# Preparing a batch's keys and values at separate places in the attention plan

## The chip, the cores and the metric

The kernel runs on one core of a Trainium2 chip. The metric is the device time of one execution in microseconds. A core has TensorE (PE, matrix products, with PEld as its weight loads), VectorE (DVE), ScalarE (ACT), GpSimd (POOL) and SyncE (SP, which here issues nearly all DMAs). Each engine takes its instructions in the order in which they were put into its queue, and waits at the head of the queue for what the instruction needs.

## The reference

Attention with keys and values that are averaged over groups of 8 positions, and an FFN behind it:

```python
k_p = k.reshape(B, H, Sp, 8, D).mean(axis=3)      # B=8, H=8, S=576, D=64, Sp=72
v_p = v.reshape(B, H, Sp, 8, D).mean(axis=3)
scores = scale * q @ k_p.T;  attn = softmax(scores);  x = attn @ v_p
x = x.transpose(0, 2, 1, 3).reshape(4608, 512)
h = x @ w_in                                      # 512 -> 2048
out = (h * clip(h + 3, 0, 6) / 6) @ w_out         # 2048 -> 512
```

## The kernel before

The 4608 tokens are cut into ten blocks of 512, 256, 384, six times 512 and 384 tokens. `run` does one block's FFN in 16 steps, one for each 128 columns of d_ff: `h` (12 matmuls into a PSUM tile `psh`, L774), `relu` on ACT and `gate` on DVE (L782, L786), `hi` on ACT and `lo` on DVE, which split the result into two fp32r parts `ghi` and `glo` (L790, L794), and two steps later `out` (L803), which adds into one PSUM tile `pso` per 128 tokens. After the last step the sums go through ACT into tiles `o` and out by DMA (L806, L808). So block 1 is a run of narrow matmuls of 256 columns, block 2 of 384, the others of 512.

While block j's FFN runs, the attention of block j+1 is fed in between its matmuls. `block_steps(j)` makes a list of attention steps for a block: for each tile of 128 tokens and each group of four heads one "scores" step (`scores`: products L412, maximum L416, exponentials L420, reciprocal of the sum L436 and L437, division on POOL L448 and L454), a transposing step three scores steps behind (`transposes`: L518, L520, then `ahi`, `alo`, `arem` by ACT and DVE, L529 to L541), and at the end of a batch's part four "av" steps (`av`, L583, which give `x`). `split_x` (L561, L562) splits x before the next block. `Paced` spreads a block's list evenly over the slots that the FFN's matmuls offer.

What the attention needs of a batch is made by side steps, which `side_steps(b)` lists. For the keys: four loads (`load_k`, L200, 288 KB each into `kst`) and four `prep_k` (a DVE reduction to `ksum`, L214, and two ACT copies into the tile `kbd`, L222). For the values: six loads (`load_v` and `load_vr`, L228 and L233; the last two are three DMAs each) and six `prep_v` (DVE reductions into `vsum`, L332; then the placing into `vhi`, `vlo` and `vrem` by ACT and DVE, L345 to L360, with two POOL memsets ahead, L318). The q tiles are loaded one tile ahead (`load_q`, L193).

`plan` joins the lists of blocks 2 to 9 into one list `every`, and hangs the side steps of batches 2 to 7 on its entries, to be done ahead of the entry. Batches 0 and 1 are prepared by hand at the start. `kbd` and the value tiles have two buffers, by the batch's parity.

Several tiles share one ring of four buffers of 128 x 576 fp32 (`ring`): raw keys, raw values, the value sums `vsum` (held from a batch's first to its last value reduction), the second half of a q tile that spans two batches (with a POOL memset, L192), and the output tiles `o`.

A scheduler puts each engine's instructions into its queue by the program's order and by when it believes them ready. Up to the fourth FFN step of block 1 the order is instead written out by hand, in `ORDER`, as numbers of an engine's instructions in program order (SP's list holds its DMAs), and `put_in_order` ties them.

Of the kernel before, what the change touches and what calls it, by code (L numbers as in the profile page):

```python
# [23 lines left out]

TLAG = 3

SIDE = 20

WSCALE = 2.0**8

# [28 lines left out]
        93 62 90 85 87 94 117-120 91 126-129 99 102 92 115 103 100 112 136 65 130 137 101 138-139 116 113 124  # L59
        121 114 125 122 140 123 143 66 63 131 64 132 134 144 135 153 133 145 141 147 142 150 148 146 154 151 149  # L60
        155 157 160 156 152 166 158 161 159 167 170-172 162-163 168 164 173 165 174 176 178 169 175 183 177
        180-181 179 187 186 184 188 185 194-197 189 202-205 198-199 182 200 208-211 190-191 201 206-207 192
        212-213 193
    """,
    "Pool": """
# [1 line left out]
    """,  # L67
    "SP": """
        2-3 1 0 4-5 8 6-7 14 9 11 10 22-24 21 20 13 12 15 18 16 19 25-26 28 31 17 27 32 34 33 29 41 30 44 51 35
        48 46 43 36 47 39 52 59 42 37-38 45 40 50 49 53-55 57-58 60-62 64 63 56  # L70
    """,
}

# [2 lines left out]
def attention_moe_kernel(  # L76
# [34 lines left out]
    for j, t in enumerate(starts):  # L111
        end, mine = t + BLOCKS[j], []
        while t < end:
            n = min(end, (t // S + 1) * S, t + (256 if j == 0 else end)) - t
# [83 lines left out]
    def load_k(b, p):  # L198
        kraw[b, p] = ring("kst")
        nc.sync.dma_start(kraw[b, p], k[b, p])  # L200
# [3 lines left out]
    def prep_k(b, p):  # L204

        two = b == 0
        if not two:
            ks = pool.tile([P, 1, SP], F32, name="ksum", bufs=1)
        elif p % 2 == 0:
            ks = ksum[p // 2] = piece(0, 2 * SP).rearrange("p (i s) -> p i s", i=2)  # L210
        else:
            ks = ksum[p // 2]
        i = p % 2 if two else 0
        nc.vector.tensor_reduce(  # L214
            out=ks[:, i], in_=kraw.pop((b, p)).rearrange("p (s o) -> p s o", o=POOL), axis=AX.X, op=ALU.add
        )
        if i == two:

            scale = 1.0 / (POOL * D**0.5)
            for h in range(2):  # L220
                rows = slice(h * D, (h + 1) * D)
                nc.scalar.mul(kbds[b % 2][rows, p - i : p + 1, h * SP : (h + 1) * SP], ks[rows], scale)  # L222
# [3 lines left out]
    def load_v(b, p):  # L226
        vraw[b, p] = ring("vst")
        nc.sync.dma_start(vraw[b, p][:, : POOL * D], v[b, p])  # L228

    def load_vr(b, g):  # L230
        vraw[b, NPAIR + g] = ring("vst")
        for c in range(3):
            nc.sync.dma_start(vraw[b, NPAIR + g][c * REM : (c + 1) * REM, : POOL * D], vr[b, g])  # L233
# [88 lines left out]
    def prep_v(b, p):  # L322


        if p == 0:
            if b not in W:
                place_v(b)
            sums = ring("vsum")[:, : (NPAIR + NG) * D]
            vsum[b] = sums.rearrange("p (c d) -> p c d", d=D)
        n = P if p < NPAIR else 3 * REM  # L330
        vs, st = vsum[b], vraw.pop((b, p))
        nc.vector.tensor_reduce(  # L332
            out=vs[:n, p], in_=st[:n, : POOL * D].rearrange("p (o d) -> p d o", o=POOL), axis=AX.X, op=ALU.add
        )
        if p == NPAIR - 1:
            place_heads(b, vs[:, :NPAIR])
        elif p == NPAIR + NG - 1:
            place_rest(b, vs[:, NPAIR:])
# [253 lines left out]
    def side_steps(b):  # L592

        ks = [lambda p=p: load_k(b, p) for p in range(NPAIR)]
        ks += [lambda p=p: prep_k(b, p) for p in range(NPAIR)]
        vs = []
        n = NPAIR + NG
        for p in range(n + 2):
            if p < n:
                vs.append(lambda p=p: load_v(b, p) if p < NPAIR else load_vr(b, p - NPAIR))  # L600
            if p >= 2:
                vs.append(lambda p=p: prep_v(b, p - 2))
        return ks, vs
# [5 lines left out]
    def block_steps(j):  # L609


        todo, steps, left = [], [], list(parts_of[j])

        def turn():
            tile, g = todo.pop(0)
            steps.append(([], lambda: transposes(j, tile, g), None, ()))
            if g == NG - 1:
                while left and (left[0][0], left[0][1] + left[0][2]) in [(b, s0 + n) for b, s0, n, _ in tile]:
                    pb, _, T, x0 = left.pop(0)
                    steps.extend(([], lambda p=p, a=(j, pb, x0, T): av(*a, p), "av", (pb,)) for p in range(NPAIR))  # L620

        for t in tiles_of[j]:
            pre = loads_behind(t)
            for g in range(NG):
                steps.append((pre, lambda t=t, g=g: scores(j, t, g), "scores", [x[0] for x in t]))
                pre = []
                todo.append((t, g))
                if len(todo) > TLAG:
                    turn()
        while todo:  # L630
            turn()
        return steps
# [259 lines left out]
    b = [Scores(t, g) for g in range(NG) for t in B]  # L892
# [77 lines left out]
    def plan():  # L970


        every = []
        for j in range(2, len(BLOCKS)):
            later_steps[j] = block_steps(j)
            every += later_steps[j]
        for b in range(2, NB):
            ends = [n for n, x in enumerate(every) if x[2] and b - 2 in x[3]]
            begin = max(ends) + 1 if ends else 0
            end = min(n for n, x in enumerate(every) if x[2] == "scores" and b in x[3])  # L980
            begin = max(begin, end - SIDE)
            ks, vs = side_steps(b)
            for n, x in enumerate(ks + vs):
                every[begin + n * (end - begin) // len(ks + vs)][0].append(x)

    plan()

    def run(steps, lag, attention, first_slot=0, preps={}):
# [88 lines left out]
```

## Time and profile before

| | |
|---|---|
| runs | 928.81 us median of 3 (928.56 to 930.24) |
| profiled execution | 929.94 us, span 928.2 us |
| PE busy | 910.8 us (98%) |
| DVE, ACT, POOL busy | 456.0 (49%), 460.3 (50%), 78.0 us (8%) |
| mean granted clock of TensorE | 0.996 |
| DMA | 57.17 MB, 62 GB/s mean |

The span is the time from the first to the last instruction; the rest of an execution lies around it. A busy share is a mean over the whole span; a stage is read from the rows of its own stretch. In a row of a timeline, the bracket holds the idle time of the engine before the instruction and what ended it.

### The profile page before, as it was taken

What the parts mean: (1) busy time and instruction counts of PE and PEld (TensorE: products, weight loads), DVE (VectorE), ACT (ScalarE), POOL (GpSimd) and SP (SyncE); (2) the same over time, 40 slices, a digit from 0 to 9 for tenths busy, and PEclk for the clock granted to TensorE, in tenths of its full rate; (3) what the DMA queues carried; (4) which work ended last, traced back from release to release, by engine and by line L of the source; (5) the groups of instructions that cost most, each with busy time, mean ns of one, the idle gap of its engine ahead of it and who ended that gap; (6) DMA issues with size and microseconds to landing.
All of it is one profiled execution on the core that took longest, in us unless ns stands there. A gap on an engine that the chain in (4) does not pass through costs nothing.

```text
span 928.2 us, 12551 instructions
## 1 busy us (share of the span) xinstructions
PE 910.8 (98%) x4500; PEld 775.8 (84%) x4500; DVE 456.0 (49%) x915; ACT 460.3 (50%) x1340; POOL 78.0 (8%) x167
## 2 busy tenths in 40 slices
PE   7899998999999999999999999999999999999997
PEld 7788887999887888888888888888888888888996
DVE  6999846564358532744354325733454224332321
ACT  5998665574446534544364435533544244333322
POOL 4100001021001100101011100110011001000000
PEclk9999999999999999999999999999999999999999
DMA  9960205040015000400050003200200000000100
GB/s 306 392 242 3 89 12 171 25 124 18 1 41 159 12 12 32 151 12 6 1 168 15 12 1 115 78 12 1 74 24 12 1 34 25 0 1 7 40 1 34
DMA packets 41790, 57.17 MB, mean 62 GB/s; under 512 B 7552, under 2 KB 23424, under 8 KB 41728
## 3 DMA queue, kind: packets, MB, share of 16 engines
q1 hardware_dynamic: 41584, 56.37, 18.9%
q8 instruction: 35, 0.57, 0.3%
q14 instruction: 27, 0.22, 0.1%
q10 hardware_dynamic: 144, 0.00, 0.0%
HBM read 46.93 MB, written 9.44 MB: 61 GB/s over the span
## 4 chain that ended last, share of the span: by engine, by line
PE 91%; DVE 3%; DMA 3%; ACT 1%; issue 1%; SPq 1%; ACTq 0%; DVEq 0%
PE psh L774 41%; PE pso L803 41%; PE psa L583 4%; PE psa L412 4%; PE psa L518 1%; DMA kst<-k_l 1%; DVE vsum L332 1%; DMA stage<-v_l 1%; PE psa L290 1%; DMA vst<-v_l 1%; DVE ksum L214 0%; PE psa L520 0%; DVE mx L416 0%; ACT o L806 0%; DMA out<-o 0%
## 5 line engine op out<-in xcount | busy, mean ns | idle before, releaser
L774 PE MATMUL psh<-xhi,w 128*128 128x512 f32 (+2 forms) x1288 | 403.3, 373 | 0.2
L803 PE MATMUL pso<-w,ghi 128*128 128x512 f32 x1152 | 363.5, 397 | 0.0
L774 PEld LDWEIGHTS psh<-xhi,w 128*128 128x128 f32 x1288 | 238.3, 189 | 37.3 <-DVE g L786 0.7
L803 PEld LDWEIGHTS pso<-w,ghi 128*128 128x128 f32 x1152 | 209.7, 188 | 36.2
L774 PE MATMUL psh<-xlo,w 128*128 128x512 f32 (+2 forms) x644 | 237.7, 369 | 0.0
L786 DVE SCALAR_TENSOR_TENSOR g<-g,psh 128x512 f32<-128x512 f32 (+2 forms) x161 | 101.4, 630 | 272.2 <-ACT g L782 271.6
L803 PE MATMUL pso<-w,glo 128*128 128x512 f32 x576 | 223.0, 393 | 0.5 <-DVE glo L794 0.5
L782 ACT ACTIVATE g<-psh,small 128x512 f32<-128x512 f32 (+2 forms) x161 | 103.7, 644 | 218.1 <-PE psh L774 204.3
L774 PEld LDWEIGHTS psh<-xlo,w 128*128 128x128 f32 x644 | 121.6, 189 | 18.6
L794 DVE TENSOR_TENSOR glo<-g,ghi 128x512 fp32r<-128x512 f32 (+2 forms) x161 | 103.4, 642 | 60.2 <-ACT ghi L790 59.0
L790 ACT CAST ghi<-g 128x512 fp32r<-128x512 f32 (+2 forms) x161 | 92.9, 577 | 76.3 <-DVE g L786 72.7
L803 PEld LDWEIGHTS pso<-w,glo 128*128 128x128 f32 x576 | 108.1, 188 | 23.3 <-DVE glo L794 0.9
L420 ACT ACTIVATE e<-psa,mx 128x72 f32<-128x72 f32 x256 | 78.5, 321 | 45.9 <-DVE mx L416 45.0
L448 POOL TENSOR_TENSOR a<-e,sm 128x256 f32<-128x256 f32 x60 | 38.1, 635 | 508.8 <-DVE sm L437 232.4
L420 ACT ACTIVATION_READ_ACCUMULATOR e<-psa,mx 128x1 f32 x256 | 52.6, 205 | 0.0
L412 PEld LDWEIGHTS psa<-kbd,qt 128*128 128x128 f32 x288 | 43.6, 191 | 4.4 <-issue 0.2
L416 DVE TENSOR_REDUCE mx<-psa 128x4 f32<-128x288 f32 x72 | 32.5, 454 | 29.2 <-PE psa L412 28.8
L412 PE MATMUL psa<-kbd,qt 128*128 128x144 f32 x288 | 46.0, 287 | 0.0
L332 DVE TENSOR_REDUCE vsum<-vst 128x64 f32<-128x512 f32 (+1 forms) x36 | 37.7, 1065 | 6.0 <-DMA vst<-vr_l 2.6
L585 ACT COPY x<-psa 128x192 f32<-128x192 f32 (+7 forms) x60 | 22.9, 387 | 31.7 <-PE psa L583 31.4
L529 ACT CAST ahi<-psa 128x256 fp32r<-128x256 f32 (+1 forms) x70 | 24.4, 350 | 25.1 <-PE psa L518 12.7
L530 DVE TENSOR_TENSOR alo<-psa,ahi 128x256 fp32r<-128x256 f32 (+1 forms) x70 | 27.4, 393 | 17.4 <-ACT ahi L529 16.7
(92 smaller groups left out, 611.4 us busy)
## 6 DMA issues: line engine op xcount, KB each, us to landing
out<-o SPq DMA_DIRECT2D x36, 256.0 KB, 2.3
raw<-w_in_l SPq DMA_DIRECT2D x16, 512.0 KB, 8.5
raw<-w_out_l SPq DMA_DIRECT2D x16, 512.0 KB, 9.2
kst<-k_l SPq DMA_DIRECT2D x28, 288.0 KB, 3.9
qt<-q_l SPq DMA_DIRECT2D x28, 256.0 KB, 3.3
vst<-v_l SPq DMA_DIRECT2D x24, 256.0 KB, 3.1
vst<-vr_l SPq DMA_DIRECT2D x36, 64.0 KB, 2.0
stage<-k_l SPq DMA_DIRECT2D x4, 288.0 KB, 3.7
```

Of the source, the lines that this page charges most:

```text
L332: nc.vector.tensor_reduce(out=vs[:n, p], in_=st[:n, : POOL * D].rearrange("p (o d) -> p d o", o=POOL), axis=AX.X, op=ALU.add)
L412: nc.tensor.matmul(to, qt[:, p, :], kbds[b % 2][:, p, :], start=r == 0, stop=r == last)
L416: nc.vector.tensor_reduce(out=self.mx, in_=self.ps, axis=AX.X, op=ALU.max, negate=True)
L420: nc.scalar.activation(self.e[:, h], self.ps[:, h], AF.Exp, bias=self.mx[:, h : h + 1], accum_out=self.sm[:, h : h + 1])
L448: engine.tensor_tensor(out=self.a[:, : 4 * D].rearrange("p (h s) -> p h s", h=4), in0=e[:, :, :D], in1=sm[:, :, None].broadcast_to([P, 4, D]),
L583: nc.tensor.matmul(ps, l, r, start=n == 0, stop=n == len(mms) - 1)
L774: nc.tensor.matmul(self.ps, l[f][:, c, :], r[:, c, :], start=c == 0 and i == 0, stop=c == NCC - 1 and i == 2)
L782: nc.scalar.activation(self.g, self.ps, AF.Relu, bias=half, scale=1.0 / (6.0 * WSCALE))
L786: nc.vector.scalar_tensor_tensor(out=g, in0=g, scalar=1.0, in1=self.ps, op0=ALU.min, op1=ALU.mult)
L790: nc.scalar.copy(self.ghi, self.g)
L794: nc.vector.tensor_tensor(out=self.glo, in0=self.g, in1=self.ghi.bitcast(F32), op=ALU.subtract)
L803: nc.tensor.matmul(pos, l, r[f], start=f == 0 and i == 0, stop=f == NF - 1 and i == 2)
```

## The change

The side steps of a batch are no longer one list of 20 that ends at the batch's first scores. The eight key steps are spread over the 12 entries before the batch's first scores entry, and the twelve value steps from that entry to the batch's first av entry. Each part begins no earlier than behind the last scores (for keys) or the last av (for values) of the batch two before. In the stretch that is ordered by hand, the four key loads of batch 2 drop out of SP's list (numbers 61 to 64 are gone, and 60 is then the q load), and on ACT instruction 192 goes ahead of 207.

```diff
-SIDE = 20
+SIDE = 12
...
-        180-181 179 187 186 184 188 185 194-197 189 202-205 198-199 182 200 208-211 190-191 201 206-207 192
+        180-181 179 187 186 184 188 185 194-197 189 202-205 198-199 182 200 208-211 190-191 201 206 192 207
         212-213 193
...
-        48 46 43 36 47 39 52 59 42 37-38 45 40 50 49 53-55 57-58 60-62 64 63 56
+        48 46 43 36 47 39 52 59 42 37-38 45 40 50 49 53-55 57-58 60 56
...
+        def uses(kind, b):
+            return [n for n, x in enumerate(every) if x[2] == kind and b in x[3]]
+
         for b in range(2, NB):
-            ends = [n for n, x in enumerate(every) if x[2] and b - 2 in x[3]]
-            begin = max(ends) + 1 if ends else 0
-            end = min(n for n, x in enumerate(every) if x[2] == "scores" and b in x[3])
-            begin = max(begin, end - SIDE)
-            ks, vs = side_steps(b)
-            for n, x in enumerate(ks + vs):
-                every[begin + n * (end - begin) // len(ks + vs)][0].append(x)
+            begin = uses("scores", b)[0]
+            for side, kind, begin, end in zip(
+                side_steps(b), ("scores", "av"), (begin - SIDE, begin), (begin, uses("av", b)[0])
+            ):
+                begin = max([begin] + [n + 1 for n in uses(kind, b - 2)])
+                for n, x in enumerate(side):
+                    every[begin + n * (end - begin) // len(side)][0].append(x)
```

## The prediction

> **What bounds the kernel now.** I read the page's busy times first, then the stretches of each FFN block, then two of these stretches instruction by instruction.
>
> ```profile
> span 928.2 us, 12551 instructions
> PE 910.8 (98%) x4500; PEld 775.8 (84%) x4500; DVE 456.0 (49%) x915; ACT 460.3 (50%) x1340; POOL 78.0 (8%) x167
> ```
>
> ```profile
> 138.00:186.00 48.00, 45.59 (x276) 40.91 (x275) 28.58 (x67) 25.64 (x84) 5.09 (x11) 0.96 0.31 95
> 186.00:262.00 76.00, 76.00 (x404) 69.13 (x403) 34.72 (x81) 40.23 (x134) 8.88 (x20) 1.00 0.15 44
> 262.00:360.00 98.00, 96.68 (x459) 79.71 (x458) 51.33 (x105) 45.40 (x147) 8.48 (x18) 1.00 0.18 53
> 360.00:459.00 99.00, 99.00 (x472) 82.78 (x471) 46.37 (x94) 46.60 (x144) 9.05 (x19) 1.00 0.15 47
> ```
>
> The window rows give length, then PE, PEld, DVE, ACT and POOL busy time, the granted clock, DMA share and GB/s; the four are the runs of FFN blocks 1 (256 tokens), 2 (384), 3 and 4 (512 each). PE is the bound, and none of its matmuls changes, so only its idle time and its clock can move. After the start-up it is idle in two of these rows alone: 48.00 - 45.59 = 2.41 us in block 1 and 98.00 - 96.68 = 1.32 us in block 3; block 1 also has the one reduced clock. Everything that can be won lies there, and a loss would be a new gap elsewhere. The first gap, closer:
>
> ```profile
> 156.00:158.00 2.00, 0.87 (x4) 0.38 (x2) 1.94 (x5) 0.78 (x3) 0.00 (x0) 1.00 0.37 91
> 158.00:160.00 2.00, 0.75 (x5) 0.59 (x6) 1.94 (x4) 1.69 (x9) 0.00 (x0) 1.00 0.50 142
> 160.00:162.00 2.00, 2.00 (x12) 2.00 (x11) 2.00 (x6) 1.33 (x4) 0.81 (x2) 0.51 0.32 94
> 162.00:164.00 2.00, 2.00 (x10) 1.81 (x9) 1.94 (x4) 0.64 (x2) 0.05 (x1) 0.63 0.08 16
> ```
>
> ```profile
> 155.06 1.07 DVE L332 TENSOR_REDUCE vsum<-vst 128x64 f32<-128x512 f32 x1 [2.33 <-DMA vst<-v_l]
> 156.47 1.03 DVE L332 TENSOR_REDUCE vsum<-vst 128x64 f32<-128x512 f32 x1
> 157.79 1.00 DVE L332 TENSOR_REDUCE vsum<-vst 128x64 f32<-128x512 f32 x1
> 158.82 0.29 DVE L541 TENSOR_TENSOR arem<-psa,arem 32x128 fp32r<-32x128 f32 x1
> 159.25 0.41 PE L518 MATMUL psa<-ident,a 128*128 128x128 f32 x2 [2.38 <-DVE arem L541]
> ```
>
> A timeline row is start, length, engine, line, operation, and in brackets the idle time before and who ended it. DVE stood 2.33 us at the head of its queue for batch 2's first values, and then did three value reductions (1.07 + 1.03 + 1.00) before the arem that frees PE. That is 5.43 us of value work ahead of arem, for a PE gap of 2.38 us, so PE had a lead of about 3.05 us over DVE here (an estimate from these rows). Behind the gap the clock is 0.51 and 0.63 for 2 us each: 2 x 0.49 + 2 x 0.37 = 1.72 us lost.
>
> The second gap, in block 3:
>
> ```profile
> 190.71 1.95 SPq L200 DMA_DIRECT2D kst<-k_l  x3
> 192.72 0.42 SPq L228 DMA_DIRECT2D vst<-v_l  x1
> ...
> 199.14 0.33 SPq L228 DMA_DIRECT2D vst<-v_l  x1
> ```
>
> ```profile
> 194.62 0.31 POOL L192 MEMSET qt<- 128x256 f32 x1 [0.91 <-DVE ksum L214]
> 272.20 3.02 DVE L332 TENSOR_REDUCE vsum<-vst 128x64 f32<-128x512 f32 x3 [0.62 <-PE psa L412]
> 279.50 1.09 ACT L806 ACTIVATE o<-pso 128x512 f32<-128x512 f32 x2
> 282.26 0.34 SPq L200 DMA_DIRECT2D kst<-k_l  x1
> 288.47 0.75 DVE L214 TENSOR_REDUCE ksum<-kst 128x72 f32<-128x576 f32 x1 [3.31 <-DMA kst<-k_l]
> 289.88 0.96 PE L803 MATMUL pso<-w,glo 128*128 128x512 f32 x3 [0.51 <-DVE glo L794]
> ```
>
> Here I read the ring of four buffers that raw keys, raw values, the value sums, the second half of a two-batch q tile and the output rows share. At 194.62 the q half-tile of the tile that spans batches 2 and 3 takes a slot, which its scores give back only at about 272. Three raw values of batch 3 (from 192.72 to 199.14) hold the others, so their sum finds no slot until 272.20. Block 2's outputs, later in program order, are copied only from 279.50. Batch 4's keys queue behind the outputs (282.26), DVE stands 3.31 us for them, glo is late and PE waits.
>
> **The change, part by part.** First the price of what is moved.
>
> ```profile
> L332 DVE TENSOR_REDUCE vsum<-vst 128x64 f32<-128x512 f32 x24 | 24.9, 1064 | 3.2 <-DMA vst<-v_l 2.5 <-PE psa L412 0.6
> L332 DVE TENSOR_REDUCE vsum<-vst 96x64 f32<-96x512 f32 x12 | 12.8, 1065 | 2.8 <-DMA vst<-vr_l 2.6
> L359 ACT ACTIVATE vrem<-vsum,small 96x128 fp32r<-96x128 f32 x24 | 7.7, 392 | 4.5 <-DVE vsum L332 4.5
> L360 DVE SCALAR_TENSOR_TENSOR vrem<-vsum,small,vrem 32x128 fp32r<-32x128 f32 x24 | 6.8, 336 | 0.2
> L346 DVE SCALAR_TENSOR_TENSOR vlo<-vsum,vhi 64x256 fp32r<-64x256 f32 x12 | 5.1, 423 | 1.9 <-POOL vlo L318 1.7
> L345 ACT ACTIVATE vhi<-vsum 64x256 fp32r<-64x256 f32 x12 | 5.0, 415 | 0.8 <-DVE sm L436 0.6
> ```
>
> *Nothing is added or removed; places move.* Per batch the values cost DVE 4 x 1.064 + 2 x 1.065 + 2 x 0.423 + 4 x 0.336 = 8.58 us, ACT 2 x 0.415 + 4 x 0.392 = 2.40 us, ten DMAs on SP (four L228, six L233) and two memsets on POOL (L318). Counting the steps of the planned list from 0 (0 to 15 run beside block 1's FFN, 16 to 35 beside block 2's), batch 2's values leave steps 6 to 15 for steps 16 to 30. Its keys go from steps 0 to 5 to steps 4 to 14. Later batches shift by some 8 to 14 steps in the same way, so that values of one batch lie beside the keys of the next.
>
> *Block 1.* DVE falls from 28.58 to 28.58 - 8.58 = 20.0 of 48 us. The wait of 2.33 us and all reductions ahead of arem go with the values. Gain: 2.38 us of PE idle and 1.72 us of clock, 4.10 in all. What is late next is the first keys:
>
> ```profile
> 142.04 5.52 SPq L200 DMA_DIRECT2D kst<-k_l  x4
> 147.65 0.56 SPq L193 DMA_DIRECT2D qt<-q_l  x1
> 148.26 0.61 SPq L808 DMA_DIRECT2D out<-o  x1
> 164.23 0.35 SPq L200 DMA_DIRECT2D kst<-k_l  x1
> ```
>
> ```profile
> 146.45 0.75 DVE L214 TENSOR_REDUCE ksum<-kst 128x72 f32<-128x576 f32 x1 [1.31 <-DMA kst<-k_l]
> ```
>
> In SP's written order the four key loads drop out, so the q load and the held-back output pass them: the keys start 0.56 + 0.61 = 1.17 us later, at about 143.2. DVE's wait for the first ksum, 1.31 us now without a PE gap, becomes some 2.5 us; queued behind it are that block's max, gate and lo operations, and PE waits for those. 2.5 is under the lead of 3.05, so nothing at best. If the load took as long as the one issued at 282.26, whose ksum starts 6.21 us later, DVE would stand until 149.4, which is 4.3 us from the 145.14 at which it fell idle (146.45 - 1.31). Minus 3.05 that is 1.2 us of PE idle. I take the middle, 0.6 us lost, because the order of DVE behind the written stretch is made anew with the loads later in it.
>
> *Block 2.* It gets 8.58 us of DVE work, 34.72 + 8.58 = 43.3 of 76 us (57%, against 60% in block 1 now), under a PE with no idle. It also gets the ten loads on SP among the q loads, and the two POOL memsets among the divisions, where POOL has 8.88 of 76 us. The lead should grow with the matmul's width: 3.05 x 384/256 = 4.6 us (estimate). One wait of 2.33 us with one reduction (1.07) stays below it; the whole old burst of 5.43 us would exceed it by 0.8 us, and with a clock drop cost 2.5 us. Bounds 0 and 2.5; I take 0, because this stretch already takes six loads of batch 3 in its first 13 us (190.71 to 199.14, above) with PE 76.00 of 76.00 busy.
>
> *Block 3.* In program order batch 3's values now come behind block 2's outputs, so they no longer hold three slots beside the q half-tile (that slots are granted in program order is my reading of the rows, no row says it). The outputs get theirs at once, and the reductions from 272.20 on are those of batch 3's values and batch 4's keys (6 + 4 = 10) instead of 6 + 4 + 6 = 16. Block 4's run has ten at its start now, four ksum and six vsum, and no idle:
>
> ```profile
> 374.08 0.75 DVE L214 TENSOR_REDUCE ksum<-kst 128x72 f32<-128x576 f32 x1
> ...
> 388.16 1.07 DVE L332 TENSOR_REDUCE vsum<-vst 96x64 f32<-96x512 f32 x1
> ```
>
> Gain 1.32 us, bounds 0 and 1.32.
>
> *Later blocks, and the rest of the written order.* They have no idle time to give and get the same ten reductions per block in another order: 0. One output copy on ACT goes ahead of one ghi cast in block 1: at most one copy's length, 0.55 us (1.09 / 2), inside the lead: 0.
>
> The sum: -2.38 - 1.72 - 1.32 + 0.6 = -4.8 us. The profiled execution took 929.94 us, its span and 1.74 us around it, and would come to 925.1. It lies 1.13 us above the median of the runs, 928.81, which comes to 924.0.
>
> The clock term deserves a doubt. The row shows half clock right behind a gap of 2.38 us. The Trainium skill, page "TensorE: Matmul & The Clock Gate", Part 1, says that the clock halves after an idle window of about 3.4 us and comes back after as much busy time; the stretch at half clock fits the second half, the gap is shorter than the first. By the page alone the dip would need another cause, and the time would be 925.7; the row has no second candidate, so I keep the 1.72.
>
> **The rivals.**
> 1. *One stall of the old size comes back*, on the first keys in block 1 or on the values in block 2. For it: DVE's waits stand at 1.31 and 3.31 us on keys already, and DVE takes its work in order. Against it: the leads above. It needs a DVE delay over 3.05 us (block 1) or 4.6 us (block 2). 924.0 - 0.6 + 4.10 = 927.5: no measurable change.
> 2. *Slower: the ring starves the values in block 2.* Value sum and q half-tile hold two of four slots, so eight loads (the last values and batch 3's keys) pass two at a time, and DVE stands before one reduction after the other. It decides where two reductions in a row each wait over 2.33 us, so that wait and work pass the 4.6 us of lead twice. Two stalls at 4.10: 923.4 + 8.2 = 931.6. Against it: the values are needed only at the last four of block 2's twenty steps.
> 3. *It doesn't do what it says.* DMA queues are not paced by steps: a batch-3 key load, due in block 2's run, goes out at 164.23 already. If values still went out and were reduced in block 1: 928.8.
> 4. *Block 3's gap stays*, because batch 4's keys still land late: 924.0 + 1.32 = 925.3.
> 5. *The clock dip isn't the gap's child* and stays: 924.0 + 1.72 = 925.7.
>
> **How the numbers follow.** My forecast 0.55, rival 1 0.14, rival 2 0.12, rival 3 0.05, rival 4 0.09, rival 5 0.05. A difference of 0.2% (1.86 us) is about what can be told from none: faster means below 926.95. So faster 0.55 + 0.09 + 0.05 = 0.69, same 0.14 + 0.05 = 0.19, slower 0.12. The range runs from the full gain without the 0.6 (923.4, and some 0.6 for scatter: 922.8) to rival 1 with 0.5 of scatter (928.0); it leaves out rivals 2 and 3.
>
> **What would show it.** Right: no vsum in 138 to 186; PE 48 of 48 busy there and clock 1.00; block 2's output copies before 272; no ksum wait over 3 us near 285. Wrong: a PE gap "<-DVE" or a second half-clock stretch in 140 to 215, with a ksum or vsum waiting for its DMA just before it.

## The result and the profile after

The changed kernel took 923.10 us (median of 6 runs, 922.26 to 926.27); the kernel before took 929.33 us in the same comparison (6 runs, 927.67 to 930.71). The ratio is 0.9937, with an interval of 0.9919 to 0.9956: 6.2 us less, where 4.8 were forecast. The profiled execution took 926.27 us, its span and 2.05 us around it, and is the slowest of the six, for a reason that lies in the start-up and is shown below.

The busy times of after, and then its stretches of blocks 1, 2 and 3, with the columns length, PE, PEld, DVE, ACT and POOL busy, granted clock, DMA share, GB/s:

```profile
span 924.2 us, 12571 instructions
PE 909.7 (98%) x4500; PEld 775.6 (84%) x4500; DVE 456.8 (49%) x915; ACT 461.8 (50%) x1340; POOL 80.9 (9%) x167
```

```profile
138.00:186.00 48.00, 48.00 (x307) 43.59 (x306) 22.95 (x60) 26.16 (x84) 6.15 (x13) 1.00 0.21 64
186.00:262.00 76.00, 76.00 (x404) 68.99 (x404) 41.30 (x93) 40.80 (x136) 8.27 (x18) 1.00 0.20 56
262.00:360.00 98.00, 98.00 (x468) 81.93 (x467) 46.57 (x96) 46.25 (x145) 8.51 (x18) 1.00 0.15 46
```

PE is busy for the whole of every row. The idle 2.41 us of block 1 and 1.32 us of block 3 are gone, the clock is 1.00 in block 1 (before 0.96), and no gap has come in their place in these rows.

The amounts are read better from one instruction that both kernels do equally often. Every FFN step has a gate (L786) that comes behind PE's sums for the step. There are 161 in each kernel, 17 in block 0 (one of its steps is done in two halves) and 16 in each other block, so the 17th, 33rd, 49th and 65th are the last of blocks 0 to 3. Timeline rows of the 17th, 49th, 65th and last gate, first of before, then of after:

```profile
124.02 0.68 DVE L786 SCALAR_TENSOR_TENSOR g<-g,psh 128x512 f32<-128x512 f32 x1
259.24 0.55 DVE L786 SCALAR_TENSOR_TENSOR g<-g,psh 128x384 f32<-128x384 f32 x1 [3.19 <-ACT g L782]
359.63 0.69 DVE L786 SCALAR_TENSOR_TENSOR g<-g,psh 128x512 f32<-128x512 f32 x1 [4.98 <-ACT g L782]
917.80 0.55 DVE L786 SCALAR_TENSOR_TENSOR g<-g,psh 128x384 f32<-128x384 f32 x1 [2.49 <-ACT g L782]
```

```profile
127.25 0.68 DVE L786 SCALAR_TENSOR_TENSOR g<-g,psh 128x512 f32<-128x512 f32 x1
257.94 0.56 DVE L786 SCALAR_TENSOR_TENSOR g<-g,psh 128x384 f32<-128x384 f32 x1 [3.19 <-ACT g L782]
355.93 0.69 DVE L786 SCALAR_TENSOR_TENSOR g<-g,psh 128x512 f32<-128x512 f32 x1 [4.99 <-ACT g L782]
914.28 0.55 DVE L786 SCALAR_TENSOR_TENSOR g<-g,psh 128x384 f32<-128x384 f32 x1 [2.49 <-ACT g L782]
```

After minus before is +3.23 at the 17th, still in block 0's FFN, then -1.30, -3.70 and -3.52. So the profiled execution of after lost 3.23 us ahead of everything that the change touches (two kernels below that leave this part as it was, with the later q load alone and with the second try beside it, lost 3.17 and 2.96 us there in theirs); blocks 1 and 2 gained 4.53, block 3 gained 2.40, and the remaining six blocks gave back 0.18 (-3.70 to -3.52). The sum over the touched part is -6.75 us, close to the -6.2 of the medians; the two profiled executions differ only by 3.67 because of the start-up. That part is in these rows of after:

```profile
34.00:36.00 2.00, 1.01 (x3) 0.84 (x3) 2.00 (x5) 1.92 (x4) 0.00 (x0) 0.66 1.07 351
36.00:38.00 2.00, 2.00 (x6) 1.59 (x5) 2.00 (x3) 1.50 (x4) 0.00 (x0) 0.50 1.03 397
38.00:40.00 2.00, 2.00 (x7) 1.72 (x7) 0.95 (x3) 1.15 (x4) 0.00 (x0) 0.50 1.03 412
40.00:42.00 2.00, 2.00 (x7) 1.53 (x7) 2.00 (x4) 1.56 (x4) 0.00 (x0) 0.63 1.02 408
```

Half clock from about 34.6 to 41.5 costs 0.68 + 1.00 + 1.00 + 0.74 = 3.42 us. In before's profile the clock is 1.00 in these four stretches, and its half clock of the start-up falls at 12 to 18 us (0.82, 0.50 and 0.83 in its three rows), where it delayed little: the profiled execution with two added reductions below, whose clock is 1.00 over all of the first 46 us, has its 17th gate only 0.41 us earlier. Single executions are therefore set against each other below by differences of gates, and kernels by their medians.

### The profile page after: what moved, and what is told of

The parts are those of the page before. It is cut to its first block, busy times and chain, and to the rows that moved or that the text cites. A ratio compares the mean times of both kernels' runs of the same rounds, so it can differ in the third digit from the quotient of the medians.

```text
span 924.2 us, 12571 instructions
## 1 busy us (share of the span) xinstructions
PE 909.7 (98%) x4500; PEld 775.6 (84%) x4500; DVE 456.8 (49%) x915; ACT 461.8 (50%) x1340; POOL 80.9 (9%) x167
## 4 chain that ended last, share of the span: by engine, by line
PE 96%; DMA 3%; DVE 1%; issue 0%; ACT 0%; SPq 0%; ACTq 0%; DVEq 0%
PE psh L774 43%; PE pso L803 43%; PE psa L583 4%; PE psa L412 4%; PE psa L518 2%; DMA raw<-w_in_l 1%; DMA raw<-w_out_l 1%; DMA stage<-k_l 1%; PE psa L520 0%; SPq L257 0%; ACT stage L420 0%; DVE u L700 0%; DVE u L689 0%; DVE stage L448 0%; ACTq L1078 0%
## 5 line engine op out<-in xcount | busy, mean ns | idle before, releaser
L803 PE MATMUL pso<-w,ghi 128*128 128x512 f32 x1152 | 364.9, 397 | 0.0
L803 PEld LDWEIGHTS pso<-w,ghi 128*128 128x128 f32 x1152 | 209.5, 188 | 36.1
L786 DVE SCALAR_TENSOR_TENSOR g<-g,psh 128x512 f32<-128x512 f32 (+2 forms) x161 | 101.4, 630 | 271.9 <-ACT g L782 270.8
L803 PE MATMUL pso<-w,glo 128*128 128x512 f32 x576 | 223.0, 392 | 0.0
L803 PEld LDWEIGHTS pso<-w,glo 128*128 128x128 f32 x576 | 108.2, 188 | 22.3
L448 POOL TENSOR_TENSOR a<-e,sm 128x256 f32<-128x256 f32 x60 | 40.3, 673 | 517.0 <-PE pso L803 180.3
L436 DVE TENSOR_SCALAR sm<-sm 128x4 f32<-128x4 f32 x72 | 12.7, 180 | 48.9 <-ACT e L420 45.1
```

The lines of the kernel that those rows point to most:

```text
L448: engine.tensor_tensor(out=self.a[:, : 4 * D].rearrange("p (h s) -> p h s", h=4), in0=e[:, :, :D], in1=sm[:, :, None].broadcast_to([P, 4, D]),
L786: nc.vector.scalar_tensor_tensor(out=g, in0=g, scalar=1.0, in1=self.ps, op0=ALU.min, op1=ALU.mult)
L803: nc.tensor.matmul(pos, l, r[f], start=f == 0 and i == 0, stop=f == NF - 1 and i == 2)
```

## The experiments

The theory after the result: two stalls, each of DVE standing in its queue before work that PE does not need yet, made up the whole gain. The rivals: the amount of DVE work in a narrow block, and the spreading of preparation as such, a little for each batch. An instruction that is tied behind another comes after it in its engine's queue. All ratios are to the kernel before, run in the same comparison.

**Only the later batches apart** (batch 2 with the loop body of before, batches 3 to 7 as in the change).

```diff
+        for b in [2]:
+            ...
-        for b in range(2, NB):
+        for b in range(3, NB):
             begin = uses("scores", b)[0]
```

> Batch 2 is prepared as before (keys and values together, in block 1's run); batches 3 to 7 as after the change. Theory (two separate gaps): block 1's gap of 2.4 us stays, with or without 1.7 us of half clock behind it; block 3's goes, because batch 3's values now come behind block 2's outputs: 1.3 to 1.8 us less than before, 927.5 to 928.0. Rival A (too much DVE work in the narrow block 1): the same here. Rival B (the gain is that bursts of key and value loads are spread out, in every block): five of six batches are spread, so five sixths of the 6.2 us, about 924.2.

Measured: 928.33 us against 929.91, ratio 0.9979 (0.9967 to 0.9991), 1.6 us less. Its stretches of blocks 1 and 3, and its 49th and 65th gate:

```profile
138.00:186.00 48.00, 45.08 (x274) 40.64 (x274) 28.59 (x67) 25.18 (x83) 5.09 (x11) 0.96 0.31 95
...
262.00:360.00 98.00, 98.00 (x469) 82.06 (x469) 46.22 (x97) 46.17 (x146) 8.54 (x18) 1.00 0.15 46
```

```profile
259.87 0.56 DVE L786 SCALAR_TENSOR_TENSOR g<-g,psh 128x384 f32<-128x384 f32 x1 [3.19 <-ACT g L782]
357.86 0.69 DVE L786 SCALAR_TENSOR_TENSOR g<-g,psh 128x512 f32<-128x512 f32 x1 [4.99 <-ACT g L782]
```

Block 1 keeps its stall (2.92 us idle and a clock of 0.96), block 3 is full. Against before the gates go from +0.63 to -1.77: block 3 alone is worth 2.40 us again, and five of six batches apart bring only that. A share for each batch would have been five sixths of 6.2 us; that rival falls.

**Block 3's stall by one load.** Before, with the q load of tile 13 (the tile with a half in the ring) hung ten steps later.

```diff
                 every[begin + n * (end - begin) // len(ks + vs)][0].append(x)
+        every[35][0].append(every[25][0].pop(0))
```

> The kernel before, with one edit: the load of the q tile that spans batches 2 and 3 is hung ten steps later (35 instead of 25), behind batch 3's value loads, so its second half no longer holds a ring slot while batch 3's values are prepared. Theory: batch 3's value sums then run in block 2 near 200 to 215 instead of at 272, block 2's outputs are copied near 266, block 3's idle of 1.32 us goes, block 1's gap stays: 927.5 to 928.0. Rival B (bursts): keys and values are loaded together as before, so nothing is won: 929.3. If the late q half itself holds up the first scores of block 3, PE gets a new gap near 262 and the time is 929 to 931.

Measured: 929.32 us, ratio 0.9989 (0.9978 to 1.0001): no gain that can be told. The mechanism is there all the same:

```profile
186.00:262.00 76.00, 75.44 (x399) 68.32 (x399) 39.91 (x91) 40.00 (x136) 8.69 (x20) 1.00 0.18 53
262.00:360.00 98.00, 98.00 (x469) 82.05 (x468) 46.24 (x96) 45.81 (x146) 9.12 (x18) 1.00 0.15 46
```

```profile
209.71 1.04 DVE L332 TENSOR_REDUCE vsum<-vst 96x64 f32<-96x512 f32 x1
211.27 0.44 PE L774 MATMUL psh<-xhi,w 128*128 128x384 f32 x1 [0.56 <-DVE g L786]
270.27 1.58 ACT L806 ACTIVATE o<-pso 128x512 f32<-128x512 f32 x3 [1.26 <-PE pso L803]
```

One q load moved behind the values, and no value or key step: block 3 is full, batch 3's values are reduced within block 2 (the last at 209.71), and block 2's outputs are copied from 270.27 instead of 279.50. So the slot of the q half-tile did hold up the values, and they the outputs and batch 4's keys. But three of the reductions now stand ahead of the gate at 210.68 in block 2, and PE is idle for 0.56 us there, so a part of the gain is given back: by the gates block 3 gains 2.41 us and block 2 loses 1.10.

**Block 1's stall by its queue, first try.** Before, with the first reduction of batch 2's values tied behind tile 6's second arem.

```diff
-        )
+        ); (b, p) == (2, 0) and behind(traced[-1], arem[all_tiles[6]])
...
-                )
+                ); arem[tile] = traced[-1].name
```

> The kernel before, with one edit: batch 2's first value reduction on DVE is tied behind the arem of the tile that is being transposed, so DVE does not stand before the late values with arem behind it. All value work stays in block 1. Theory: the 2.38 us gap near 157 goes, and the half clock behind it where it falls; block 3's gap stays: 2.4 to 4.1 us less than before, 925.2 to 926.9. Rival A (too much DVE work in block 1, 28.6 of 48 us): the wait only moves and PE is as late a little later, 928.5 to 929.5. Rival B (bursts of loads): no change, 929.3.

Measured: 929.65 us, ratio 0.9993 (0.9981 to 1.0005). It missed, and DVE's rows tell why:

```profile
156.22 1.06 DVE L332 TENSOR_REDUCE vsum<-vst 128x64 f32<-128x512 f32 x1 [2.42 <-DMA vst<-v_l]
157.31 0.29 DVE L541 TENSOR_TENSOR arem<-psa,arem 32x128 fp32r<-32x128 f32 x1
157.63 1.05 DVE L332 TENSOR_REDUCE vsum<-vst 128x64 f32<-128x512 f32 x1
...
159.09 1.00 DVE L332 TENSOR_REDUCE vsum<-vst 128x64 f32<-128x512 f32 x1
160.01 0.41 DVE L786 SCALAR_TENSOR_TENSOR g<-g,psh 128x256 f32<-128x256 f32 x1
160.47 0.58 PE L774 MATMUL psh<-xhi,w 128*128 128x256 f32 x1 [1.86 <-DVE g L786]
```

Only one reduction was tied, and the next took its place at the head of the queue. DVE still stood 2.42 us, and three reductions still came ahead of the gate at 160.01: 0.49 us of PE idle before the arem and 1.86 before the gate took the place of 2.38 at the arem.

**Both single edits together** gave as little:

> The edits of the last two together, on the kernel before; keys and values of each batch stay together. Theory: both gaps go without the change, so the time is that of the changed kernel within 1 us: 923.1 to 924.5. Rivals A and B: most of the gap to the changed kernel remains, 927 to 929.

Measured: 929.40 us, ratio 0.9996 (0.9983 to 1.0009). It missed too. Block 3 is full again (98.00 of 98 us), but block 1 has 45.70 of 48 at a clock of 0.96, as with the first try, and block 2 has 75.43 of 76, as with the later q load.

**Block 1's stall by its queue, second try.** Every reduction of batch 2's values is tied behind the glo that was written last before it in program order; all of them stay in block 1.

```diff
-        )
+        ); b == 2 and behind(traced[-1], late[0])
...
-            nc.vector.tensor_tensor(out=self.glo, ..., op=ALU.subtract)
+            nc.vector.tensor_tensor(out=self.glo, ..., op=ALU.subtract); late[:] = [traced[-1].name]
```

> The kernel before, with all six reductions of batch 2's values left in block 1 but each held in VectorE's queue behind the glo that was traced last before it, so that the first of them comes after tile 6's arem, mx and a gate and none stands before unlanded values ahead of what TensorE needs. All work stays in block 1. Theory (the wait in the queue, not the amount of work): TensorE's gap of 2.4 us in block 1 goes, and with it the half clock behind it; block 3's gap stays. That is 2.4 to 4.1 us less than before: 925.5 to 927.6, ratio 0.9955 to 0.9975. Rival A (too much VectorE work for the narrow block of 256 tokens): a gap of 1.5 us or more stays in block 1, 928.5 to 930, ratio 0.9985 to 1.001.

Measured: 925.21 us against 929.48, ratio 0.9950 (0.9935 to 0.9966), 4.3 us less. Its three stretches, and the start of its value work:

```profile
138.00:186.00 48.00, 47.98 (x299) 43.33 (x298) 29.89 (x69) 27.95 (x88) 6.03 (x13) 1.00 0.32 95
186.00:262.00 76.00, 75.48 (x401) 68.31 (x401) 35.18 (x81) 38.97 (x134) 7.80 (x18) 1.00 0.15 44
262.00:360.00 98.00, 97.41 (x460) 80.47 (x459) 53.49 (x107) 47.00 (x149) 8.49 (x18) 1.00 0.18 53
```

```profile
153.55 0.28 DVE L541 TENSOR_TENSOR arem<-psa,arem 32x128 fp32r<-32x128 f32 x1
154.16 0.29 DVE L541 TENSOR_TENSOR arem<-psa,arem 32x128 fp32r<-32x128 f32 x1 [0.33 <-ACT arem L540]
157.07 1.07 DVE L332 TENSOR_REDUCE vsum<-vst 128x64 f32<-128x512 f32 x1
```

This is the clearest run. DVE does more in block 1 than before (29.89 us in that stretch against 28.58), and PE is full, at full clock: the two arem go first, and the reduction at 157.07 finds its data there and waits for nothing. The amount of work in the narrow block was not the matter; that rival falls. The time came out 0.3 us below the expected range. By the gates block 1 alone gained 4.48 us, more than the 4.1 that its idle time and its clock promised; block 3, which lost less than before (0.59 us idle against 1.32), gained 1.01, and block 2, where a gate now comes late (0.52 us idle), lost 0.85.

**That and the later q load together.**

> The kernel before with both single edits: batch 2's six reductions held behind a glo each, and tile 13's query loads hung at step 35 in place of step 25. No preparation moves to another block by program order. Theory (two stalls make up the whole gain): both gaps go, a gap of about 0.5 us appears in block 2 as it did with the query loads alone, and the time comes within 1.5 us of the changed kernel: 923 to 926, ratio 0.993 to 0.996. Rival A (the spreading of keys and values itself is worth something beside the stalls): 926.5 or more.

Measured: 926.29 us, ratio 0.9957 (0.9941 to 0.9973), between the two expectations. Blocks 1 and 3 are full, but block 2 has 74.59 of 76 us: three gates came late there, 0.52, 0.20 and 0.69 us, where half a microsecond was expected; by the gates block 2 loses 2.25. Filling block 3 this way crowds block 2, and the kernel with block 1 alone mended is no worse. The changed kernel fills all three stretches; these edits do not.

**Which batches need it.** The changed kernel with the loop body of before for the later batches, first for 4 to 7 (shown), then for 5 to 7.

```diff
-        for b in range(2, NB):
+        for b in range(2, 4):
...
+        for b in range(4, NB):
+            ends = [n for n, x in enumerate(every) if x[2] and b - 2 in x[3]]
...
```

> The changed kernel with batches 4 to 7 prepared as before (keys and values together ahead of the scores) and batches 2 and 3 alone apart. Theory (the gain is two stalls, at batches 2 and 3): the changed kernel's time, 922.5 to 924.5, ratio to before 0.9925 to 0.9948. Rival B (a gain from each batch): two sixths of 6.2 us, about 927.3, ratio near 0.998.

> The changed kernel with batches 2, 3 and 4 apart and batches 5 to 7 prepared as before. With only batches 2 and 3 apart, TensorE lost 1.40 us in block 3 again, where batch 3's values met all of batch 4. Theory (the gain is in the stalls of blocks 1 and 3, and block 3's has two parents, batch 3's values and batch 4's undivided preparation): now blocks 1, 2 and 3 are full as in the changed kernel, block 4 on may lose a little where batch 4's values meet batch 5; ratio to before 0.9925 to 0.9948, 922.5 to 925. Rival B (each batch that is still together costs its share of the gain): three sixths of 6.2 us, ratio 0.9967, about 926.4, with gaps in the later blocks.

Measured: 925.54 us with two batches apart (ratio 0.9951, 0.9937 to 0.9965) and 924.84 with three (0.9950, 0.9937 to 0.9964, against 929.87). The first missed both expectations, and its rows of block 3 say most of why:

```profile
262.00:360.00 98.00, 96.60 (x458) 80.15 (x457) 52.97 (x105) 46.77 (x143) 8.07 (x18) 1.00 0.21 61
```

```profile
284.65 0.75 DVE L214 TENSOR_REDUCE ksum<-kst 128x72 f32<-128x576 f32 x1 [2.05 <-DMA kst<-k_l]
286.80 3.03 DVE L332 TENSOR_REDUCE vsum<-vst 128x64 f32<-128x512 f32 x3
290.70 1.04 DVE L332 TENSOR_REDUCE vsum<-vst 128x64 f32<-128x512 f32 x1
291.64 0.69 DVE L794 TENSOR_TENSOR glo<-g,ghi 128x512 fp32r<-128x512 f32 x1
292.34 0.30 PE L583 MATMUL psa<-ahi,vhi 128*128 128x64 f32 x1 [1.13 <-DVE glo L794]
```

Batch 3's values have moved into block 3, and there they meet keys and values of batch 4 together: DVE is busy 52.97 us, stands 2.05 us for a key, and its value reductions delay a glo. By the gates block 3 gains 0.43 us over before, where the changed kernel gains 2.40; blocks 1 and 2 gain 3.95 (for 4.53), with 0.43 us of PE idle before a gate in block 1. Block 3's stall thus has two parents, and batch 4 must be apart too. With three batches apart blocks 1 to 3 are full (48.00, 76.00 and 98.00 us), and block 4 lacks 0.34 us; the time lies in the expected range, the ratio just above it (0.9950 for 0.9948). From the 17th gate to the last this kernel gains 6.43 us on before, the full change 6.75. Dividing batches 5 to 7 brings nothing that the times can tell. From the 81st gate to the last, the four kernels that divide them (the changed one, the one with only the later batches apart, and the two below) give back 0.17 to 0.20 us against before, and the other seven -0.01 to 0.03.

**The same delay by work instead of a wait.** The changed kernel with one, then two, reductions of weights that have long been there, ahead of tile 6's second arem.

```diff
-                nc.scalar.copy(rem[: 2 * REM, o], mine)
+                nc.scalar.copy(rem[: 2 * REM, o], mine); (tile, r) == (all_tiles[6], 1) and delay(...)
```

> The changed kernel with one added reduction on VectorE directly ahead of the second arem of tile 6 in block 1. It reads 2048 elements of weights long in the chip's memory and waits for no load; by the value reductions' 1.065 us for 512 elements it should last about 4.2 us (an estimate). Its result is not used. Theory (whatever holds VectorE there longer than its lead on TensorE shows as a gap, a wait or work alike): a gap of 4.2 less about 3 us, 0.5 to 2 us, in block 1; the time 0.5 to 2 us over the changed kernel, or up to 3.7 if the clock falls behind the gap: 923.5 to 927. Rival A (only the load's wait matters, or the lead is far longer): no gap above 0.3 us, 922.5 to 923.5.

> The changed kernel with two of the added reductions ahead of tile 6's second arem in block 1 in place of one, with a glo and an mx between them in the queue: 2 x 2.29 + 0.27 us of work and those two instructions, some 5.5 us more ahead of arem than in the changed kernel. With one (2.55 us of work) TensorE had no gap. Theory (a hold of VectorE there is free up to a lead of about 3 us and costs its excess beyond): a gap of 1.5 to 3 us in block 1 with VectorE's arem or a gate as its end, without any wait for a load; 925.5 to 930. Rival A (only waits for loads bite): no gap above 0.3 us in block 1, within 0.7 us of the kernel with one.

Measured: 925.42 us with one (ratio 0.9952, 0.9935 to 0.9969), 927.52 with two (0.9978, 0.9967 to 0.9990). The size of one was misjudged: it took 2.29 us, not 4.2, so together with a short one of 0.27 it stayed inside the lead, and block 1 has 48.00 of 48 us. Its time lies in the theory's range for another reason, which stands below. With two:

```profile
155.85 0.27 DVE L462 TENSOR_REDUCE spare<-arem 32x1 f32<-32x128 f32 x1
156.15 2.29 DVE L462 TENSOR_REDUCE spare<-w 128x4 f32<-128x2048 f32 x1
...
159.06 2.27 DVE L462 TENSOR_REDUCE spare<-w 128x4 f32<-128x2048 f32 x1
161.34 0.29 DVE L541 TENSOR_TENSOR arem<-psa,arem 32x128 fp32r<-32x128 f32 x1
160.65 0.41 PE L518 MATMUL psa<-ident,a 128*128 128x128 f32 x2 [1.09 <-ACT e L420]
161.69 0.44 PE L518 MATMUL psa<-ident,a 128*128 128x128 f32 x2 [0.52 <-DVE arem L541]
```

From 155.85 to 161.34 DVE holds the arem back for 5.49 us without any wait for a load, and PE stands 1.09 + 0.52 = 1.61 us. The first of these waits is ended by ACT's exponentials, which were late behind a maximum that stands between the two reductions in DVE's queue. So a hold by work costs about as much as one by a wait, beyond a lead of some 5.49 - 1.61 = 3.9 us. Counted in the same way, before held its arem back from 155.06 - 2.33 = 152.73 to 158.82, 6.09 us, for an idle time of 2.38, which is a lead of 3.7. And 2.55 us of work cost nothing in block 1. Another 0.81 us of PE went in block 2 (75.19 of 76). The kernel with one reduction showed the stall in another place, in block 2, where DVE's order came out differently from the changed kernel's:

```profile
194.47 1.02 DVE L332 TENSOR_REDUCE vsum<-vst 128x64 f32<-128x512 f32 x1 [1.08 <-DMA vst<-v_l]
...
196.00 0.45 PE L774 MATMUL psh<-xhi,w 128*128 128x384 f32 x1 [1.16 <-DVE g L786]
```

From 190.85 to the gate at 195.41 three value reductions and a wait of 1.08 us fill DVE's queue there, and PE loses 1.16 us.

## Why the prediction was right, point by point

- *Block 1, -2.38 of idle.* Right, and shown from both sides: the gap goes with the values (the change) or with their place in the queue alone (the second try), and stays without either. The term is a little small: blocks 1 and 2 gained 4.53 us by the gates, 0.43 more than the 4.10 of idle and clock together. DVE is busy for 22.95 us in that stretch, not 20.0, while PE does more there (307 matmul records against 276). What the change's two edits of the written order are worth by themselves, no run shows.
- *The clock, -1.72, and rival 5.* With the gap gone the clock is 1.00 in block 1 in the change and in the second try. How firm the tie is, is less certain than I made it: idle of 2.92, of 0.49 + 1.86 and even of 1.09 + 0.52 us brought 0.96 too, but 2.10 + 0.31 us in the run with the later q load brought none (clock 1.00 in block 1). Nor does every execution of before have the dip: of the 35 that the first four experiments were compared with, four show a mean clock of 1.000 (a loss of 1.72 us would make it 0.998), with 928.69 us on average against the median of 929.91. The Trainium skill, page "TensorE: Matmul & The Clock Gate", Part 1, says that the clock follows the activity in a free-running window of about 3.4 us, whose phase differs from run to run. Here the loss of 1.72 us at half clock is a stretch of 3.44 us, and the start-up's 3.42 us is two of them, so the length agrees. Its rule that idle of about 3.4 us is needed does not agree with 1.61 us in two pieces. The term belongs in the sum as a likely cost, not as a fixed one.
- *The first keys, +0.6.* Not lost. The keys came later than forecast, and DVE stood twice:

```profile
147.07 1.06 SPq L200 DMA_DIRECT2D kst<-k_l  x1
148.88 1.55 SPq L200 DMA_DIRECT2D kst<-k_l  x3
...
150.90 0.75 DVE L214 TENSOR_REDUCE ksum<-kst 128x72 f32<-128x576 f32 x1 [1.29 <-DMA kst<-k_l]
154.08 0.75 DVE L214 TENSOR_REDUCE ksum<-kst 128x72 f32<-128x576 f32 x1 [2.09 <-DMA kst<-k_l]
```

  The start-up's 3.23 us taken off, the first key goes out 1.80 us later than before (forecast 1.17). Waits of 1.29 and 2.09 us with a gate between them passed without a PE gap. This is the middle of a range whose lower end, nothing, was the true one, and it is part of why the gain was larger than forecast.
- *Block 2, 0.* Right for the change: PE 76.00 of 76, DVE 41.30 us where 43.3 were forecast, value sums from 193.82 to 206.30 and waits of 0.78 and 0.18 us among them. The lead of 4.6 us that I gave this block by the width of its matmuls is not borne out: two of the kernels above lost 0.56 and 1.16 us there behind three reductions each, the second with a hold of 195.41 - 190.85 = 4.56 us, which leaves a lead of about 3.4 us. In the change no more than two value sums stand between one gate or glo and the next.
- *Block 3, -1.32.* The mechanism is right, and the reading that slots are granted in program order fits: the q load alone, moved, let values, outputs and keys through. In the change the outputs are copied from 265.84 (before 279.50), and batch 4's keys are summed from 281.18 without a wait for a load. The term was mis-sized: by the gates it is 2.40 us, in the change as in the kernel with only the later batches apart. Idle time understates a stall. One L803 matmul of 512 columns is recorded with 0.39 us, but three in a row take 0.84 where nothing holds them, so records overlap and one starts every 0.23 us. In before:

```profile
266.72 0.84 PE L803 MATMUL pso<-w,glo 128*128 128x512 f32 x3
...
288.51 0.86 PE L803 MATMUL pso<-w,ghi 128*128 128x512 f32 x3
```

  The second row stands right ahead of the gap that the prediction shows at 289.88. The next matmul would have started at 288.51 + 3 x 0.23 = 289.20. It started at 289.88, 0.68 us late for 0.51 shown as idle, and its own row of three takes 0.96 instead of 0.84, so the gap cost about 0.8. By starts in this way the four gaps of block 3 (0.13, 0.51, 0.58 and 0.10 us of idle) cost 0.40, 0.78, 0.84 and 0.17 us, 2.2 together, which leaves only 0.2 of the 2.40 open.
- *Rivals.* No stall of the old size came back (1), the ring did not starve the values (2), the values did leave block 1 (3: the first sum of batch 2 is at 193.82, none in the stretch 138 to 186), block 3's gap went (4). Rival 1's mechanism is real, as the run with one added reduction shows; the changed order misses it.
- *The sum.* -4.8 forecast, -6.75 by the gates, -6.2 by the medians: 0.6 that was not lost, 1.1 in block 3 and 0.4 in blocks 1 and 2 beyond what was counted from idle and clock, less 0.18 later. The misses nearly all point one way: 923.10 lies below 923.4, the full gain that the prediction reckoned with, and is inside its range only by the 0.6 us allowed for scatter.

## What to carry to other kernels

On an engine that takes its work in order, look for early work that stands before unlanded data ahead of what the bounding engine needs next: moving it behind that work in the queue can bring most of the gain without moving it to another stage, but tie every instruction of the kind, or the next one takes the place. When a shared ring holds things of different lifetimes, follow its slots in program order, since one long holder can delay outputs and loads two stages on. Measure a stall by the shift of an instruction that both kernels have, not by the idle time alone.

## What the runs showed of the hardware that was not expected

- The half clock of the start-up has no fixed place: at 12 to 18 us in before's profile, at 34 to 42 us in after's, behind much the same gaps (0.98 us at 34.83 in before, 0.99 us at 35.03 in after). In the second place it costs over 3 us, half of what the change brings.
- A reduction of 2048 values per partition read in a row, into 4 sums, took 2.29 us, 1.1 ns each. The key reductions (L214), whose 8 members lie side by side, took 0.75 us for 576 values, 1.3 ns each, and the value reductions, also of 8 members but 64 values apart, 1.065 us for 512, 2.1 ns each. No run here varies that order alone.
